# Value products of the late heads in 64x64 tiles only: three blocks of 64 keys, one row tile of the group on each half of the rows

## The chip, the cores and the metric

The kernel runs on one core of one Trainium2 chip. The metric is the device time of one execution in microseconds (us). Before the change it is 658.24 us, the median of three runs (657.96 to 659.07).

## The reference

The kernel computes an attention with a causal window and a few global keys, and passes its result through a two-layer network with an ELU between the layers. All of it is f32. The mask of every row lets through the 96 keys up to its own and the first 8 keys.

```python
scores = q @ k.T / sqrt(64) - slope[h] * dist           # B=4, H=8, S=768, D=64
scores = where(is_global | is_local, scores, -1e9)      # 8 global keys, 96 local ones
a = softmax(scores)
x = (a @ v) -> [B * S, H * D]                           # 3072 x 512
h = x @ w_in                                            # 512 x 2048
g = where(h > 0, h, exp(min(h, 0)) - 1)
out = g @ w_out                                         # 2048 x 512
```

## The kernel before, in words

**Groups and heads.** The 3072 rows are cut into 12 groups of 256 rows: two row tiles i of 128 rows (`NT = 2`). A row tile has two halves r of 64 rows (`HW`). Each half looks at 168 keys (`LW`): 64 own ones, 96 before them and 8 global ones. Heads go in pairs j = 0, 1, so a group has four pairs `hp`.

**Early and late groups.** The first three groups are prepared in `pair` and `heads32`, where TensorE transposes the probabilities. The other nine groups, 36 head pairs, are the late ones (`far`), and the change is in these. A late pair k goes through the engines as follows.
- `visit` puts it on TensorE. A visit first does the value products of the pair that was scored two visits earlier (`BEHIND = 2`), and then the scores of its own pair (`scores`, L468). Both write the same two PSUM banks `s`, one for each row tile or head.
- `turned` takes the scores on: softmax on VectorE and ScalarE (L456, L458), division on GpSimd (L577), and a transpose of 32x32 blocks on VectorE into the tile `tr` (L582). `tr` has six blocks (`BLK = 6`) of 32 keys; 168 keys are padded to 192.
- The 32x32 transpose leaves the keys of a block on 32 partitions of a quadrant. To bring them into the order that a matmul needs, `tr` is stored to a buffer `dd` in DRAM (L591, two stores: blocks 0 to 3 and blocks 4, 5) and read back. Blocks 0 to 3 come back as `pt`, 128 keys on 128 partitions (L596, one transfer). Blocks 4 and 5 come back as `pu`, 64 keys of the first row tile on partitions 0 to 63 and of the second on 64 to 127 (L603, two transfers).
- `values` multiplies: eight matmuls over 128 keys (L617, array tiles of 128 rows x 64 columns, two heads side by side), then eight over the other 64 keys (L622, array tiles of 64x64; four of them, two row tiles and two heads, lie in the array at once).
- `v` holds the values of the first 128 keys, loaded for each pair; `u` holds those of the rest, loaded once for two pairs (L550, L553).

**Rest of TensorE's work.** The network of the earlier groups runs between the visits: `moe` (L844 up, L870 down), and from the sixth group on `seven` (L722 up, L778 down), which loads prepared sums of weights `mix` from DRAM (L761).

**What sets the order.** Every operation is handed to `Plan.add` with a cost, a due time and what it reads and writes. `Plan.order` then lays out all engines greedily by its own model of durations, DMA bandwidth and free buffers (`SLOTS`). The order on each engine is fixed when the program is built. SyncE (SP) issues nearly all DMAs, in order: one that waits holds up those behind it.

Of the kernel before, what the change touches and what calls it, by code (L numbers as in the profile page):

```python
# [16 lines left out]
P = 128  # L17
NG = 8
NL = P - NG
NT = 2  # L20
HW = P // 2
BACKW = 96
LW = HW + BACKW + NG
BLK = 6
# [12 lines left out]
VN = 2 * VC  # L37

# [185 lines left out]
def sp():  # L224
    return (("SP", 450.0, False),)
# [19 lines left out]
class Kernel:  # L245
# [290 lines left out]
    def far(self, b, gi, hp, xh, xl, due, end, X):  # L536


        nc, p = self.nc, self.plan
        qk = self.sb("qk", "qk", [P, W + KS], slots=X.get("qk"))  # L540
        src = self.qkv[b, gi, hp]
        p.add(sp(), lambda e: nc.sync.dma_start(qk.t, src[:, :W + KS]), writes=[qk], due=due - 14000, nbytes=P * (W + KS) * 4)
        sc = self.scale.t[:, hp:hp + 1]
        p.add(act(W) + dve(W, True) + (("POOL", 60 + 1.1 * W, True),), lambda e: self.scaled(e, qk.t[:, :W], qk.t[:, :W], sc), [qk], [qk], due - 8000, slack=self.LOADED)
        rest = []

        def chain(ss, after):
            rest.extend(self.turned(b, hp, gi * NT, ss, due, end, X, after))
            v = self.sb("v", "v", [P, VC], slots=X.get("v"))
            p.add(sp(), lambda e: nc.sync.dma_start(v.t, src[:, W + KS:W + KS + VC]), writes=[v], due=end - 9000, nbytes=P * VC * 4)  # L550
            if hp % 2 == 0:
                self.rest = u = self.sb("u", "u", [P, VC], slots=X.get("u"))
                p.add(sp(), lambda e: nc.sync.dma_start(u.t, src[:, W + KS + VC:]), writes=[u], due=end - 9000, nbytes=P * VC * 4)  # L553
            rest.extend((v, self.rest))

        return qk, chain, (rest, hp, xh, xl, end)

    def turned(self, b, hp, t0, ss, due, end, X, after):
# [4 lines left out]
        pt, pu = self.sb("pt4", "pt4", [P, 4, NT, 2, 32], slots=X.get("pt4")), self.sb("pu", "pu", [P, 4, 2, 32])  # L563
# [21 lines left out]
        outs = []  # L585
        for a, (w0, w1) in enumerate(((0, 4), (4, BLK))):
            w = w1 - w0
            at = slice(P * w0, P * w1)
# [4 lines left out]
            outs.append(p.add(sp(), out, [tr], [dd], due - 2000, nbytes=P * w * 512, beside=tuple(outs)))  # L593
        def back(e):
# [3 lines left out]
        p.add(sp(), back, [dd], [pt], due - 1900, nbytes=P * 2048)  # L598
        backs = []
        for i in range(NT):  # L600
            def back(e, i=i):
                src = dd.t[P * 4:].rearrange("(q k w) x -> (k w) q x", q=4, w=2)[:, :, i * HW:(i + 1) * HW]
                nc.sync.dma_start(pu.t[i * HW:(i + 1) * HW].rearrange("k q j t -> k q (j t)"), src)  # L603

            backs.append(p.add(sp(), back, [dd], [pu], due - 1890, nbytes=P * 512, beside=tuple(backs)))
        return pt, pu

    def values(self, rest, hp, ss):

        pt, pu, v, u = rest  # L610
        vx = v.t.rearrange("p (i r j d) -> p i r j d", i=NT, r=2, j=2)
        ux = u.t.rearrange("p (m r j d) -> p m r j d", m=2, r=2, j=2)
        out = lambda i, r, j: ss[i].t[j * HW:(j + 1) * HW, r, LW:LW + HW].rearrange("p (c t) -> p c t", c=2)
        for i in range(NT):
            for r in range(2):
                for j in range(2):
                    self.nc.tensor.matmul(out(i, r, j), vx[:, i, r, j], pt.t[:, 2 * r:2 * r + 2, i, j], start=r == 0, stop=False)  # L617
        for r in range(2):
            for j in range(2):
                for i in range(NT):  # L620
                    rows = slice(i * HW, (i + 1) * HW)
                    self.nc.tensor.matmul(out(i, r, j), ux[rows, hp % 2, r, j], pu.t[rows, 2 * r:2 * r + 2, j], start=False, stop=r == 1)  # L622

    def visit(self, k, due):


        nc, p, N = self.nc, self.plan, len(self.fars)
        reads, cost = [], 250.0
        new = old = None
        if k < N:  # L630
            new = self.far(*self.fars[k][:-2], due, *self.fars[k][-2:])
            self.open.append(new[2])
            reads += [new[0]]
            cost += 575.0
        if k >= self.BEHIND:
            old = self.open[k - self.BEHIND]
            reads += old[0]
            cost += 660.0
        ss = [self.bank("s", "s", [P, NT, 2 * P]) for _ in range(2)]

        def both(e):
            if old:
                self.values(old[0], old[1], ss)
# [269 lines left out]
    def build(self):  # L913
# [63 lines left out]
        for _, f in sorted(todo, key=lambda x: x[0]):  # L977
# [29 lines left out]
             "gl": ["gl0", "gl1", "gl2"], "io": ["io0", "io1", "io2", "io3"], "part": [f"pa{i}" for i in range(6)], "mix": [f"pa{i}" for i in range(6)], "pu": ["pu0", "pu1"], "hl": ["x0", "ph2"], "tf": ["tf0", "tf1", "tf2", "tf3"],  # L1007
# [226 lines left out]
def layouts(q, k, v, w_in, w_out):  # L1234
# [9 lines left out]
    vf = np.zeros((B, nb, H // 2, 2 * NT, P, 2, D), np.float32)  # L1244
    tile_of = lambda x, t: x[:, :, t * P:(t + 1) * P]
    for g in range(nb):
        prev = max(g * NT - 1, 0)
        x = [tile_of(k, prev)[:, :, P - BACKW:]]
        for i in range(NT):
# [5 lines left out]
            for r in range(2):  # L1255
                x1 = y[:, :, r * HW:r * HW + LW].reshape(B, H // 2, 2, LW, D).swapaxes(2, 3)
                vv[:, g, :, :, 0, i, r] = x1[:, :, :P]
                for m in range(2):
                    vv[:, g, ::2, (2 - m) * HW - (LW - P):(2 - m) * HW, 1, i, r] = x1[:, m::2, P:]
            vf[:, g, :, 2 * i:2 * i + 2] = y.reshape(B, H // 2, 2, 2, 2, 2, 32, D).transpose(0, 1, 3, 4, 6, 5, 2, 7).reshape(B, H // 2, 2, P, 2, D)  # L1260
        kf[:, g] = np.concatenate(x, axis=2).reshape(B, H // 2, 2, KS, D).transpose(0, 1, 4, 2, 3)
    at = np.arange(P)
    first = at % 4 * 32 + at // 4
    key = at % 2 * 32 + at % HW // 2
    vp = vv[..., :NT, :, :, :][:, :, :, first].copy()
    vp[:, :, :, :, 0] = vv[:, :, :, first, 0]
    for m in range(2):
        x = np.zeros_like(vv[:, :, ::2, :HW, 1])
        x[:, :, :, :LW - P] = vv[:, :, ::2, (2 - m) * HW - (LW - P):(2 - m) * HW, 1]
        x = x[:, :, :, key[:HW]]  # L1270
        for i in range(NT):
            vp[:, :, ::2, i * HW:(i + 1) * HW, 1, m] = x[:, :, :, :, i]
    halves = lambda x: x.reshape(B, nb, H // 2, D, 2, -1).swapaxes(3, 4).reshape(B, nb, H // 2, 2 * D, -1)
    qkv, qkv1 = (np.concatenate([halves(qT), halves(kf), x], axis=4)
                 for x in (vp.reshape(B, nb, H // 2, P, VN), vv.reshape(B, nb, H // 2, P, VN)))
# [30 lines left out]
```

## Time and profile before

| what | value |
|---|---|
| median of three runs | 658.24 us |
| the profiled execution's own time | 657.76 us |
| its span, first to last instruction | 655.9 us |
| granted TensorE clock, mean | 0.995 |
| TensorE busy | 640.3 us (98%) |
| VectorE busy | 488.9 us (75%) |
| ScalarE busy | 418.3 us (64%) |
| DMA moved | 143.43 MB, 107837 packets, 27744 of them under 512 B |

The profiled execution has 1.9 us around its span. A matmul in f32 stands in the trace as two records: L617 has 576 records for 36 x 8 matmuls. PE is TensorE's matmul side, PEld its weight loads, SPq the queue that SyncE issues. A busy PE is not a PE at its peak: the ends of the records are modelled and they overlap, so durations on PE are read from start to start.

### The profile page before, as it was taken

To read this page: it belongs to the slowest core of one execution; us is meant where nothing else is said; L and a number is where in the kernel's file an instruction comes from. 1 tells how busy PE (TensorE), PEld (TensorE's weight loads), DVE (VectorE), ACT (ScalarE), POOL (GpSimd) and SP (SyncE) were. 2 spreads that over 40 slices of the span, in tenths; PEclk is the share of its full clock that TensorE was granted. 3 is DMA by queue.
4 is the path that set the end of the run, shared out by engine and by line. 5 is a ranking of instruction groups with operands and counts; after the bars stand their busy time and mean duration, and the time that the engine had idled before them with its cause. 6 is when DMAs were issued, how large, how long until landed. Compare 5 with 4: busy or idle time off the path is not lost.

```text
span 655.9 us, 17768 instructions
## 1 busy us (share of the span) xinstructions
PE 640.3 (98%) x6390; PEld 583.9 (89%) x6390; DVE 488.9 (75%) x1611; ACT 418.3 (64%) x1218; POOL 192.7 (29%) x480
## 2 busy tenths in 40 slices
PE   8989999999999999999999999999999999999996
PEld 5768888989887888888999999999999999999995
DVE  6998998897787777644767876877877867866655
ACT  6898886765655666655666675676675676655452
POOL 3565475544266455221113121121121121110000
PEclk9999999999999999999999999999999999999999
DMA  8989373200288658676588889798788789774542
GB/s 310 363 298 406 136 270 80 66 16 17 90 254 279 196 191 272 229 233 184 178 251 284 258 265 264 238 284 262 247 275 255 250 271 267 228 224 152 176 146 83
DMA packets 107837, 143.43 MB, mean 219 GB/s; under 512 B 27744, under 2 KB 55136, under 8 KB 107744
## 3 DMA queue, kind: packets, MB, share of 16 engines
q1 hardware_dynamic: 107744, 142.25, 67.3%
q8 instruction: 51, 0.84, 0.5%
q14 instruction: 42, 0.34, 0.2%
HBM read 111.28 MB, written 30.93 MB: 217 GB/s over the span
## 4 chain that ended last, share of the span: by engine, by line
PE 80%; DVE 6%; DMA 6%; ACT 3%; issue 2%; POOL 2%; SPq 1%; DVEq 0%; POOLq 0%; ACTq 0%
PE h L722 23%; PE o L778 20%; PE o L870 13%; PE h L844 13%; PE s L468 4%; PE s L617 3%; DMA qk<-in_qkv_dram 2%; PE s L622 2%; DMA dd<-tr 2%; PE pv L501 1%; DMA pt<-dd 1%; ACT pr L458 1%; POOL pr L577 1%; PE t L521 1%; DVE mix L307 1%
## 5 line engine op out<-in xcount | busy, mean ns | idle before, releaser
L577 POOL TENSOR_SCALAR pr<-pr,st 128x168 f32<-128x168 f32 x144 | 66.5, 461 | 269.3 <-DVE st L476 222.2
L722 PE MATMUL h<-xh,w 128*128 128x256 f32 x896 | 124.3, 280 | 0.0
L722 PEld LDWEIGHTS h<-xh,w 128*128 128x128 f32 x896 | 113.1, 188 | 2.7 <-DVE gg L732 1.9
L844 PEld LDWEIGHTS h<-xh,w 128*128 128x128 f32 x640 | 95.9, 188 | 15.9 <-DVE gl L307 3.7
L844 PE MATMUL h<-xh,w 128*128 128x256 f32 x640 | 102.1, 283 | 1.5 <-DVE gl L307 1.3
L870 PE MATMUL o<-w,gh 128*128 128x512 f32 x320 | 102.7, 403 | 0.3
L732 DVE SCALAR_TENSOR_TENSOR gg<-e,h 128x256 f32<-128x256 f32 x112 | 47.0, 419 | 68.9 <-ACT e L731 68.1
L458 ACT ACTIVATE pr<-pr,nmax 128x168 f32<-128x168 f32 x192 | 82.2, 429 | 14.4 <-DVE nmax L456 13.9
L730 ACT ACTIVATE e<-h 128x256 f32<-128x256 f32 x112 | 42.9, 383 | 59.8 <-PE h L722 59.8
L722 PE MATMUL h<-xl,w 128*128 128x256 f32 x448 | 71.1, 280 | 0.0
L456 DVE CUSTOM_DVE_ANT_0 pr<-s,far 128x168 f32<-128x168 f32 x192 | 54.2, 326 | 17.3 <-ACT xh L299 13.7
L870 PEld LDWEIGHTS o<-w,gh 128*128 128x128 f32 x320 | 54.3, 190 | 10.2 <-issue 1.4
L307 POOL TENSOR_TENSOR w<-g,w 128x256 fp32r<-128x256 f32 x64 | 50.4, 811 | 42.5 <-ACT w L299 27.6
L722 PEld LDWEIGHTS h<-xl,w 128*128 128x128 f32 x448 | 60.5, 188 | 0.9 <-issue 0.7
L852 DVE SCALAR_TENSOR_TENSOR h<-e,h 128x256 f32<-128x256 f32 x80 | 33.8, 422 | 32.4 <-ACT e L851 32.1
L778 PE MATMUL o<-mix,sh 128*128 128x256 f32 x336 | 57.5, 279 | 0.0
L870 PE MATMUL o<-w,gl 128*128 128x512 f32 x160 | 56.0, 403 | 0.0
L582 DVE STREAM_TRANSPOSE tr<-pr 128x192 f32<-128x192 f32 x144 | 49.3, 362 | 3.7 <-POOL pr L577 2.7
L850 ACT ACTIVATE e<-h 128x256 f32<-128x256 f32 x80 | 30.6, 383 | 33.5 <-PE h L844 33.0
L299 ACT CAST sh<-sum 128x512 fp32r<-128x512 f32 x56 | 34.8, 621 | 25.0 <-DVE sum L746 25.0
L844 PE MATMUL h<-xl,w 128*128 128x256 f32 x320 | 50.7, 280 | 0.0
L778 PE MATMUL o<-w,sh 128*128 128x256 f32 x336 | 48.8, 280 | 0.7 <-DVE ob L808 0.7
(129 smaller groups left out, 1299.9 us busy)
## 6 DMA issues: line engine op xcount, KB each, us to landing
mix<-mixed SPq DMA_DIRECT2D x168, 256.0 KB, 4.0
qk<-in_qkv_dram SPq DMA_DIRECT2D x48, 312.0 KB, 3.7
v<-in_qkv_dram SPq DMA_DIRECT2D x48, 256.0 KB, 4.4
dd<-tr SPq DMA_DIRECT2D x36, 256.0 KB, 3.5
pt<-dd SPq DMA_DIRECT2D x36, 256.0 KB, 4.0
bits<-in_w_in_dram SPq DMA_DIRECT2D x16, 512.0 KB, 7.7
bits<-in_w_out_dram SPq DMA_DIRECT2D x16, 512.0 KB, 8.9
mixed<-mix SPq DMA_DIRECT2D x32, 256.0 KB, 3.0
```

The source lines that it names most:

```text
L299: self.nc.scalar.copy(out, x)
L307: self.on(e).tensor_tensor(out, x, y, ALU.subtract)
L456: first = p.add((("DVE", 85 + 1.042 * LW, False),), lambda e: nc.vector.tensor_tensor_reduce(x(), s.t[:, i, :LW], tab, -(2.0 ** -(h + 1)), ...
L458: p.add(act(LW, extra=200), lambda e: nc.scalar.activation(x(), x(), AF.Exp, bias=nm, scale=-1.0, accum_out=st.t[:, n, 0:1]), [pr], [pr, s ...
L577: nc.gpsimd.tensor_scalar(pr.t[:, :LW], pr.t[:, :LW], st.t[:, n, 3:4], 1.0, ALU.mult, ALU.mult)
L582: nc.vector.transpose(tr.t[:, :, i, j], pr.t.rearrange("p (b r) -> p b r", r=32))
L722: nc.tensor.matmul(h.t, w1.t[:, s, cc * P:(cc + 1) * P], x.t[:, cc], start=n == 0 and s == HI and cc == 0, stop=n == 1 and cc == self.NCC - 1)
L730: p.add(act(W, True), lambda e: nc.scalar.activation(ex.t, h.t, AF.Relu, scale=-1.0), [h], [ex], d - 8000)
L732: p.add(dve(W), lambda e: nc.vector.scalar_tensor_tensor(gs(), ex.t, -1.0, h.t, ALU.add, ALU.max), [h, ex], [g], d - 8000)
L778: nc.tensor.matmul(acc[bank].t[:, half], a, b.t[:, LO if t == 1 else HI, x], start=j == 0 and t == 0 and n in first, stop=j == self.NFC // ...
L844: nc.tensor.matmul(h.t, w1.t[:, s, cc * P:(cc + 1) * P], x.t[:, cc], start=n == 0 and cc == 0, stop=n == 2 and cc == self.NCC - 1)
L870: nc.tensor.matmul(o.t[:, :at.stop - at.start], g.t[:, i * P:(i + 1) * P], w2.t[:, s, at], start=fc == f0 and n == 0 and s == HI, stop=fc ...
```

## The change

The 168 keys of a late pair, padded to 192, are taken as three blocks of 64 instead of one of 128 and one of 64. Row tile i of the group lies on partitions 64i to 64i + 63, for all three blocks.
- `values` has 24 matmuls of 64x64 tiles instead of eight of 128x64 and eight of 64x64.
- `tr` goes out in one store (L584 after the change) of 1 KB pieces, and comes back in two transfers (L591 after the change), one for each row tile, all in pieces of 256 B.
- `pu` and `u` are gone; `pt4` and `v` are half again as large. The values are laid out on the host to match.
- The planner's cost of the value products in a visit goes from 660 to 640 ns, and two of the four buffers of `tf` are now the ones that `u` had.

```diff
@@ chain, in far @@
-            rest.extend(self.turned(b, hp, gi * NT, ss, due, end, X, after))
-            v = self.sb("v", "v", [P, VC], slots=X.get("v"))
-            p.add(sp(), lambda e: nc.sync.dma_start(v.t, src[:, W + KS:W + KS + VC]), writes=[v], due=end - 9000, nbytes=P * VC * 4)
-            if hp % 2 == 0:
-                self.rest = u = self.sb("u", "u", [P, VC], slots=X.get("u"))
-                p.add(sp(), lambda e: nc.sync.dma_start(u.t, src[:, W + KS + VC:]), writes=[u], due=end - 9000, nbytes=P * VC * 4)
-            rest.extend((v, self.rest))
+            rest.append(self.turned(b, hp, gi * NT, ss, due, end, X, after))
+            v = self.sb("v", "v", [P, VL], slots=X.get("v"))
+            p.add(sp(), lambda e: nc.sync.dma_start(v.t, src[:, W + KS:]), writes=[v], due=end - 9000, nbytes=P * VL * 4)
+            rest.append(v)
@@ turned @@
-        pt, pu = self.sb("pt4", "pt4", [P, 4, NT, 2, 32], slots=X.get("pt4")), self.sb("pu", "pu", [P, 4, 2, 32])
+        pt = self.sb("pt4", "pt4", [P, BLK // 2, 4, 2, 32], slots=X.get("pt4"))
...
-            def out(e, w0=w0, w1=w1, w=w, at=at):
-                nc.sync.dma_start(dd.t[at].rearrange("(p w) x -> p (w x)", w=w), tr.t[:, w0:w1].rearrange("p w i j r -> p (w i j r)"))
+        def out(e):
+            nc.sync.dma_start(dd.t.rearrange("(a p w) x -> p a (w x)", a=BLK // 2, w=2), tr.t.rearrange("p (a w) i j r -> p a (w i j r)", w=2))
...
-            src = dd.t[:P * 4].rearrange("(q k w) x -> (k w) q x", q=4, w=4)
-            nc.sync.dma_start(pt.t.rearrange("k q i j t -> k q (i j t)"), src)
...
-                src = dd.t[P * 4:].rearrange("(q k w) x -> (k w) q x", q=4, w=2)[:, :, i * HW:(i + 1) * HW]
-                nc.sync.dma_start(pu.t[i * HW:(i + 1) * HW].rearrange("k q j t -> k q (j t)"), src)
+                src = dd.t.rearrange("(a q k w) x -> (k w) (a q) x", a=BLK // 2, q=4, w=2)[:, :, i * HW:(i + 1) * HW]
+                nc.sync.dma_start(pt.t[i * HW:(i + 1) * HW].rearrange("k a q j t -> k (a q) (j t)"), src)
@@ values @@
-        for i in range(NT):
+        for a in range(BLK // 2):
             for r in range(2):
                 for j in range(2):
-                    self.nc.tensor.matmul(out(i, r, j), vx[:, i, r, j], pt.t[:, 2 * r:2 * r + 2, i, j], start=r == 0, stop=False)
-        for r in range(2):
-            for j in range(2):
-                for i in range(NT):
-                    rows = slice(i * HW, (i + 1) * HW)
-                    self.nc.tensor.matmul(out(i, r, j), ux[rows, hp % 2, r, j], pu.t[rows, 2 * r:2 * r + 2, j], start=False, stop=r == 1)
+                    for i in range(NT):
+                        y = slice(i * HW, (i + 1) * HW)
+                        self.nc.tensor.matmul(ss[i].t[j * HW:(j + 1) * HW, r, LW:LW + HW].rearrange("p (c t) -> p c t", c=2), vx[y, a, r, j],
+                                              pt.t[y, a, 2 * r:2 * r + 2, j], start=(a, r) == (0, 0), stop=(a, r) == (BLK // 2 - 1, 1))
@@ visit @@
-            cost += 660.0
+            cost += 640.0
@@ SLOTS @@
-"pu": ["pu0", "pu1"], "tf": ["tf0", "tf1", "tf2", "tf3"],
+"tf": ["tf0", "tf1", "rk0", "va0"],
```

The planner lays the program out anew. On TensorE most visits keep their place between the blocks of the network. These are the rows of TensorE around the visit that does the value products of late pair 20 (the one whose products begin at 395.39 us before), first before the change:

```order
L722 MATMUL h_6413<-xh_5065,w_521_2228 128x256 x8
L722 MATMUL h_6413<-xl_5106,w_521_2228 128x256 x4
L617 MATMUL s_6435<-pt_1257_6333,v_6118 64x64 x4
L617 MATMUL s_6436<-pt_1257_6333,v_6118 64x64 x4
L622 MATMUL s_6435<-pu_6341,u_5587 64x64
L622 MATMUL s_6436<-pu_6341,u_5587 64x64
```

And the same place after it, with the first two of its 24 matmuls (L706 is the line that was L722, L605 the new matmul):

```order
L706 MATMUL h_6483<-xh_5111,w_513_2239 128x256 x8
L706 MATMUL h_6483<-xl_5152,w_513_2239 128x256 x4
L706 MATMUL h_6504<-xh_5111,w_519_2275 128x256 x8
L605 MATMUL s_6519<-pt_1228_6404,v_6187 64x64
L605 MATMUL s_6520<-pt_1228_6404,v_6187 64x64
```

One more block of eight matmuls of the network now stands ahead of this visit. The same holds for the value products that begin at 445.01, 494.51 and 544.02 us before. The other visits from 255 us on keep their places.

On SyncE's queue, these are the rows around the store and the return of late pair 27 before the change, from the last `mix` load ahead of them to the first behind:

```order
L761 DMA mix_7847<-mixed_3508 128x512
L591 DMA dd_7858<-tr_7804 128x512
L591 DMA dd_7858<-tr_7804 128x256
L542 DMA qk_7903<-in_qkv_dram 128x624
L550 DMA v_7906<-in_qkv_dram 128x512
L596 DMA pt_1555_7916<-dd_7858 128x4x128
L603 DMA pu_7927<-dd_7858 64x4x64 x2
L553 DMA u_7947<-in_qkv_dram 128x512
L761 DMA mix_7950<-mixed_3748 128x512
```

And after it:

```order
L745 DMA mix_7941<-mixed_3539 128x512
L584 DMA dd_7952<-tr_7898 128x3x256
L543 DMA qk_8004<-in_qkv_dram 128x624
L551 DMA v_8007<-in_qkv_dram 128x768
L591 DMA pt_1516_8017<-dd_7952 64x12x64 x2
L745 DMA mix_8046<-mixed_3780 128x512
```

Between the two `mix` loads eight issues become five (`x2` counts as two); what stands ahead of and behind them is the same.

## Rows read from the trace of the kernel before

**Rows 1.** The page, part 1: busy us, share of the span and instructions

```profile
PE   640.3 (98%) x6390; PEld 583.9 (89%) x6390; DVE 488.9 (75%) x1611; ACT 418.3 (64%) x1218; POOL 192.7 (29%) x480
```

**Rows 2.** A stretch of late visits: us, busy by engine, granted clock, DMA share, GB/s

```profile
475.00:525.00 50.00, 49.95 (x565) 48.15 (x566) 37.18 (x136) 32.55 (x94) 7.67 (x32) 1.00 0.83 260
```

**Rows 3.** Line view of L617: ns min/median/max, first and last start us

```profile
L617 PE MATMUL s<-pt,v x576: 222/222/271, 108.3 to 592.8; 128*64 128x64 f32 x192
```

**Rows 4.** Timeline of PE, one visit: start us, us, line, operation, records

```profile
425.61 0.69 PE L617 MATMUL s<-pt,v 128*64 128x64 f32 x16
426.23 0.46 PE L622 MATMUL s<-pu,u 64*64 64x64 f32 x16
426.51 0.75 PE L468 MATMUL s<-qk 64*64 64x168 f32 x16
427.19 1.21 PE L722 MATMUL h<-xh,w 128*128 128x256 f32 x8
```

**Rows 5.** Timeline of PE, narrow windows around 426.24: what runs there

```profile
426.01 0.29 PE L617 MATMUL s<-pt,v 128*64 128x64 f32 x4
426.23 0.29 PE L622 MATMUL s<-pu,u 64*64 64x64 f32 x4
...
426.07 0.23 PE L617 MATMUL s<-pt,v 128*64 128x64 f32 x2
```

**Rows 6.** Timeline of PE, narrow windows: entry into 64x64, and into 128x64

```profile
98.58 0.40 PE L844 MATMUL h<-xh,w 128*128 128x256 f32 x2
98.91 0.37 PE L468 MATMUL s<-qk 64*64 64x168 f32 x4
...
107.96 0.40 PE L844 MATMUL h<-xh,w 128*128 128x256 f32 x2
108.29 0.34 PE L617 MATMUL s<-pt,v 128*64 128x64 f32 x4
```

**Rows 7.** Line view of the round trip's issues on SyncE: ns min/median/max

```profile
L591 SPq DMA_DIRECT2D dd<-tr x72: 319/424/1354, 93.2 to 583.7; - x72
L603 SPq DMA_DIRECT2D pu<-dd x72: 585/607/1690, 96.2 to 587.9; - x72
L596 SPq DMA_DIRECT2D pt<-dd x36: 370/377/861, 95.7 to 586.7; - x36
```

**Rows 8.** Timeline of SyncE's queue, round trip of late pair 27

```profile
474.10 0.85 SPq L591 DMA_DIRECT2D dd<-tr  x2
...
477.15 1.25 SPq L550 DMA_DIRECT2D v<-in_qkv_dram  x1
478.49 0.39 SPq L596 DMA_DIRECT2D pt<-dd  x1
478.97 1.24 SPq L603 DMA_DIRECT2D pu<-dd  x2
```

**Rows 9.** DMA issues: count, KB each, median us from issue to landing

```profile
pt<-dd SPq DMA_DIRECT2D x36, 256.0 KB, 4.0
...
pu<-dd SPq DMA_DIRECT2D x72, 64.0 KB, 3.7
```

**Rows 10.** View of tile pu, 479 to 481: issues of pair 27, landing

```profile
L603 SPq DMA_DIRECT2D pu<-dd x2: 585/596/607, 479.0 to 479.6; - x2
...
DMA to landing us min/median/max: 3.7/3.9/4.1
```

**Rows 11.** View of tile pu, 488.5 to 491: issues of pair 28, landing

```profile
L603 SPq DMA_DIRECT2D pu<-dd x2: 585/597/609, 488.7 to 489.4; - x2
...
DMA to landing us min/median/max: 5.8/6.0/6.2
```

**Rows 12.** Timeline of PE: the value products of pairs 27 and 28 begin

```profile
483.49 0.28 PE L617 MATMUL s<-pt,v 128*64 128x64 f32 x2
...
494.51 0.28 PE L617 MATMUL s<-pt,v 128*64 128x64 f32 x2
```

**Rows 13.** Timeline of PE: the visit that waits for pu

```profile
338.92 0.40 PE L622 MATMUL s<-pu,u 64*64 64x64 f32 x11 [0.34 <-DMA pu<-dd]
```

More of the change, by code (lines that the diff above doesn't have):

```diff
@@ L37 @@
 VN = 2 * VC
+VL = BLK // 2 * 2 * P
 class Tl:
@@ L584, in turned @@
             p.add((("DVE", 150 + 1.042 * 32 * BLK, False),), turn, [pr], [tr], due - 2500 + 10 * n, slack=300.0)
[L585 to L588, printed above, removed]
-            def out(e, w0=w0, w1=w1, w=w, at=at):
-                nc.sync.dma_start(dd.t[at].rearrange("(p w) x -> p (w x)", w=w), tr.t[:, w0:w1].rearrange("p w i j r -> p (w i j r)"))
-            outs.append(p.add(sp(), out, [tr], [dd], due - 2000, nbytes=P * w * 512, beside=tuple(outs)))
-        def back(e):
-            src = dd.t[:P * 4].rearrange("(q k w) x -> (k w) q x", q=4, w=4)
-            nc.sync.dma_start(pt.t.rearrange("k q i j t -> k q (i j t)"), src)
-        p.add(sp(), back, [dd], [pt], due - 1900, nbytes=P * 2048)
+        def out(e):
+            nc.sync.dma_start(dd.t.rearrange("(a p w) x -> p a (w x)", a=BLK // 2, w=2), tr.t.rearrange("p (a w) i j r -> p a (w i j r)", w=2))
+        p.add(sp(), out, [tr], [dd], due - 2000, nbytes=P * BLK * 512)
         backs = []
@@ L642, in both @@
             if old:
-                self.values(old[0], old[1], ss)
+                self.values(old[0], ss)
             if new:
@@ L1006 @@
              "x": ["x0"], "xh": ["xh0", "xh1", "xh2"], "xl": ["xl0", "xl1", "xl2"], "e": ["e0", "e1"], "gh": ["gh0", "gh1", "gh2"],
-             "gl": ["gl0", "gl1", "gl2"], "io": ["io0", "io1", "io2", "io3"], "part": [f"pa{i}" for i in range(6)], "mix": [f"pa{i}" for i in range(6)], "pu": ["pu0", "pu1"], "hl": ["x0", "ph2"], "tf": ["tf0", "tf1", "tf2", "tf3"],
+             "gl": ["gl0", "gl1", "gl2"], "io": ["io0", "io1", "io2", "io3"], "part": [f"pa{i}" for i in range(6)], "mix": [f"pa{i}" for i in range(6)],  "hl": ["x0", "ph2"], "tf": ["tf0", "tf1", "rk0", "va0"],
              "g": ["io2", "io3"], "sum7": ["ph2", "x0"], "rh": ["gh0", "gh1"], "rl": ["gl0", "gl1"], "sh": ["xh2", "xl2"], "o2": ["v0"], "o3": ["t0"]}
@@ L1257, in layouts @@
                 vv[:, g, :, :, 0, i, r] = x1[:, :, :P]
+                keys[:, g, :, i, :LW, r] = x1
                 for m in range(2):
                     vv[:, g, ::2, (2 - m) * HW - (LW - P):(2 - m) * HW, 1, i, r] = x1[:, m::2, P:]
-            vf[:, g, :, 2 * i:2 * i + 2] = y.reshape(B, H // 2, 2, 2, 2, 2, 32, D).transpose(0, 1, 3, 4, 6, 5, 2, 7).reshape(B, H // 2, 2, P, 2, D)
         kf[:, g] = np.concatenate(x, axis=2).reshape(B, H // 2, 2, KS, D).transpose(0, 1, 4, 2, 3)
[L1262 to L1272, printed above, removed]
+    late = keys.reshape(B, nb, H // 2, NT, BLK // 2, 2, 32, 2, 2, D).transpose(0, 1, 2, 3, 6, 5, 4, 7, 8, 9)
     halves = lambda x: x.reshape(B, nb, H // 2, D, 2, -1).swapaxes(3, 4).reshape(B, nb, H // 2, 2 * D, -1)
     qkv, qkv1 = (np.concatenate([halves(qT), halves(kf), x], axis=4)
-                 for x in (vp.reshape(B, nb, H // 2, P, VN), vv.reshape(B, nb, H // 2, P, VN)))
+                 for x in (late.reshape(B, nb, H // 2, P, VL), vv.reshape(B, nb, H // 2, P, VN)))
     dm, ff = w_in.shape
```

14 lines of the change are left out of this document (6 added, 8 removed).

## The prediction

> **What bounds the kernel now.** I read the page's first part, then a stretch of late visits, then the value products: their line, the timeline of one visit, and the DMA round trip that feeds them. The reader is to see in the first that TensorE is busy for 640.3 of 655.9 us, with VectorE at 75% and ScalarE at 64% [rows 1]. Among the late visits it is tighter still: 49.95 of 50 us, at a granted clock of 1.00 (the 2.4 GHz level), with the DMA engines 0.83 busy [rows 2]. So what TensorE does faster shortens the kernel one for one, as long as nothing it needs comes late; and what comes late costs as much. All sums are made against the profiled execution's 657.76 us, 655.9 of span and 1.9 around it. The median of the runs, 658.24, lies 0.48 higher; I add that at the end.
>
> **TensorE's part: minus 5.0 us.** L617 has 576 records, 36 visits with 16 each, two for a matmul [rows 3]; L622 has as many. L617's records begin two at a time, the two heads; L622's four at a time, two heads and two row tiles [rows 5]. Call such a set a round: before there are 8 rounds of L617 and 4 of L622. After, 24 matmuls give 48 records, in the order L622 had, so 12 rounds of four. The number of rounds stays 12. What goes is one change of the array's shape, from 128x64 to 64x64, inside each visit.
>
> In the visit shown L617 begins at 425.61, L622 at 426.23 and the scores at 426.51, so the products take 0.62 + 0.28 = 0.90 us [rows 4]. L617's last rounds begin at 426.01 and 426.07, a step of 0.06, but L622's first comes only at 426.23, 0.16 later [rows 5]: 0.10 for the change of shape. After it four rounds need 0.28 instead of 4 x 0.06 = 0.24, so the first round costs 0.04 more, and that goes as well. Afterwards: four rounds with the slow first one, 0.28, and eight at 0.06, 0.48, together 0.76. That is 0.14 a visit, and 36 x 0.14 = 5.0 us. From below, if the 0.04 stays, 36 x 0.10 = 3.6. From above, if the whole 0.16 goes, 5.8. The value is the middle one, since all its pieces are read from one visit.
>
> The entry into the visit now is 128x128 to 64x64 instead of 128x128 to 128x64. The early visits without products show it: from the next to last record of the network to the first of L468 it is 98.91 - 98.58 = 0.33 us, and to L617 108.29 - 107.96 = 0.33 [rows 6]. Nothing is gained or lost there. The planner's 20 ns less for a visit moves no block but those named below.
>
> **The round trip: issues.** SyncE issues two stores (0.85 us with the pause), then `pt` (0.39) and two `pu` (1.24) for pair 27 [rows 8]. One store less saves about 0.42, its median [rows 7]. The return becomes two issues instead of three, each with 64 partitions and 12 pieces of 256 B per partition, where `pu` had 4. No row shows such a shape. From below each costs what `pu` costs at least, 0.585; from above three times `pu`'s median, 1.82, as the pieces are three times as many [rows 7]. I take `pu`'s 0.61: `pt` has 512 pieces and is issued in 0.377, `pu` has half as many and needs 0.607, so the time does not go by the number of pieces. The return then takes 1.3 us to issue instead of 478.49 to 480.21, 1.7. Against that stand 1536 pieces instead of 1024, and 196 KB in each issue. `pt` needs 4.0 us to land for 256 KB, `pu` 3.7 for 64 [rows 9]; I put 3.7 + 0.5 behind the last issue. The start of the return may not follow the store at once: in rows 8 the load of `v`, held for 1.25 us, ends at 478.40 and `pt` is issued behind it; I count half the store's 0.42. Sum: -0.2 - 0.4 + 0.5 = -0.1 us, with -0.5 and about +2 as its ends (+2: two issues of 1.82 are 3.6, 1.9 more than now). The queue behind the return holds `mix` loads, which are late by as much or little.
>
> **The round trip: how late it may be.** Before, `pu` is needed 0.62 us after the products begin [rows 4]; after, the first round needs both transfers whole. The visit between a pair's scores and its products is also 0.14 shorter. So the deadline comes 0.76 earlier. I compared, for all 36 pairs, the last landing of `pu` with the start of the products. In 22 it lands 1.4 us or more ahead. The other 14 lie between 1.0 ahead and 1.2 behind. Pair 27 is one: issued at 479.6, landed 3.7 later, at 483.3 [rows 10], products at 483.49 [rows 12]. Pair 28 is another: 489.4 + 5.8 = 495.2 [rows 11], products at 494.51, so 0.7 behind, just hidden by L617 [rows 12]. One does wait: after L622's first records TensorE stands until 338.92 [rows 13]. All such delays come to 0.8 us by the same comparison.
>
> The new order puts a block of eight matmuls, 0.94 us, ahead of the products of pairs 20, 24, 28 and 32, which are the four with `pu` 0.2 to 0.8 behind in this way. They come out even or better. With an unchanged round trip I get waits of 2.0 us: pair 15 alone 1.35, the rest from pairs 8, 11, 19, 31 with 0.05 to 0.35; a wait of one pair gives the next one time, so a couple of pairs counts once. At -0.1 they are about 1.6, at the low end of -0.5 0.9, nearly all of it pair 15. Less the 0.8 of today that is +0.8 and +0.1. I take +0.5, between the two, since the comparison holds to a tenth or two only.
>
> **Other edits.** `v` comes as 384 KB for a pair instead of 256 and, for every second, 256 more: the same bytes. That is half an issue less for a pair. `tf` keeps four buffers. VectorE, ScalarE and GpSimd do the same operations, some in other places. These I cost at 0: they lie beside TensorE's stream, with VectorE at 75% and ScalarE at 64% [rows 1]. If that cover were gone in each visit, because the shorter products leave them 0.14 us less, it would cost the same 36 x 0.14 = 5.0 us.
>
> Sum: 657.76 - 5.0 + 0.5 = 653.3, and on the scale of the median 653.7 us.
>
> **The Trainium skill against this.** The trace has `pu`, in 256 B pieces, land in 3.7 us and `pt`, in 512 B ones, in 4.0 [rows 9]: small pieces cost nothing to be seen at 64 KB. The Trainium skill's page "DMA: Bandwidth & Descriptors" (Specifications) puts the least size for full rate at 512 B and says that the engines read, modify and write below it. All of the return is now below it; by that rule the first rival is the outcome, at its time. The trace neither shows nor excludes it at 196 KB.
>
> The second is about the feed. In the visit 48 records begin within 427.19 - 425.61 = 1.58 us, 33 ns each [rows 4]. The Trainium skill's page "TensorE: Matmul & The Clock Gate" (Wait — 56ns, not 53.3ns?) says that the sequencer spends about 62 ns on a matmul when it decodes in software. The trace disagrees over one visit; whether a queue filled earlier hides it there, no row shows. That is the third rival.
>
> **Rivals.**
> 1. *The return comes late (slower).* Its issues take 1.0 us each or more, or its small pieces land later, and each couple of tight pairs makes TensorE wait. At 1.0 us beyond today the waits are 7 couples or single pairs with 0.3 to 2.3 us, together 9, less 0.8: 657.76 - 5.0 + 8.2 = 661.0, or 661.4 on the median's scale. It decides from about +0.65 on, where the waits eat the 5.0. For it: DMA engines 0.83 busy, 14 thin pairs. Against: one store and one return issue less, and `pt`'s quick issue.
> 2. *Half eaten.* The round trip is 0.3 to 0.6 longer; waits of 3 to 5 us. At 0.45: 657.76 - 5.0 + 3.7 = 656.5, or 657.0.
> 3. *The feed is the limit.* 72 records at 33 ns are 2.37 us instead of 1.58 - 0.14 = 1.44: 36 x 0.93 = 33 us more than the forecast, 687. Against it: L622's 16 records begin within 0.28 us [rows 4].
> 4. *It does not do what it says.* The 0.16 step is not the change of shape but something that remains, such as the weights' first load in the new place: 658.2, no change. Against it: the same 0.16 is there in all visits that do not wait.
>
> **How the numbers follow.** Chances: forecast 0.63, rival 1 0.15, rival 2 0.16, rival 3 0.02, rival 4 0.04. A measurement of this kernel tells 0.2%, 1.3 us, from no change. Faster: the forecast and half of rival 2, 0.71. Same: the other half and rival 4, 0.12. Slower: 0.17. The range goes from 651.9 (5.8 saved and the 0.5 not spent) to 659.0, which takes in rival 2 and the mild part of rival 1. The forecast's own range is 651.9 to 655.
>
> **What would show it.** In the profile after, a visit's products take 0.76 us from L605's first record to the scores and 36 of them are alike: that shows the first step. The return's issues at 0.6 us each, and waits of TensorE for `pt` of 1 to 2 us in all, show the second. Issues above 1 us, or waits for `pt` above 5 us in sum, would make the prediction wrong.

## The result, and the profile after

The changed kernel takes 661.98 us (median of its runs, 659.41 to 664.29) where before took 658.24. The ratio is 1.0067, with a 95% interval of 1.0045 to 1.009: slower by 0.67%, or 4.4 us on 658.24. The forecast was 653.7 us and faster, and 661.98 lies outside the range too. Only the first rival gave a time of this size, 661.4. The profiled execution took 661.4 us with a span of 659.6, against 655.9 of span before.

The first part of the page after, which answers to [rows 1] (busy us and share):

```profile
PE 638.4 (97%) x6966; PEld 584.2 (89%) x6966; DVE 484.1 (73%) x1613; ACT 416.6 (63%) x1214; POOL 191.8 (29%) x482
```

TensorE has 1.9 us less work in a span that is 3.7 us longer. What a visit costs when nothing is late, TensorE's timeline shows for one of them (late pair 26; start us, us, line, operation, records), beside [rows 4]:

```profile
477.70 0.93 PE L605 MATMUL s<-pt,v 64*64 64x64 f32 x48
478.45 0.75 PE L469 MATMUL s<-qk 64*64 64x168 f32 x16
479.13 1.21 PE L706 MATMUL h<-xh,w 128*128 128x256 f32 x8
```

The products now run from 477.70 to 478.45: 0.75 us where there were 0.90. In the records all undisturbed visits agree (0.748 to 0.749 against 0.896 to 0.897; the last two, which have no scores behind them, 0.86 against 1.01). So 0.148 us a visit went, 5.3 in all. The saving is there.

The waits view of TensorE after shows what took it back (us in all, times, longest; "issue" is a wait for which the profile names nothing):

```profile
PE s L605 <- DMA pt<-dd: 7.3, 11, 1.0
...
PE s L605 <- issue: 0.6, 1, 0.6
```

The same view of the kernel before, which the prediction had only as a comparison of landings:

```profile
PE h L844 <- DVE gl L307: 1.3, 1, 1.3
...
PE s L617 <- DMA pt<-dd: 0.4, 1, 0.4
PE s L622 <- DMA pu<-dd: 0.3, 1, 0.3
```

Waits for the return grew from 0.7 to 7.3 us. The account: from a visit's first product to the end of its scores the 36 visits sum to 60.28 us instead of 56.83, and the steps ahead of them to 10.09 instead of 8.61; together +4.9, in spite of the 5.3 saved. The 1.3 us that an up block waited for VectorE before (L844) are not there after. That makes +3.6 of the 3.7. (In one experiment, e9, the profiled execution was disturbed; nothing is read from its trace.)

One waiting visit, late pair 24, from TensorE's timeline after:

```profile
447.66 0.32 PE L605 MATMUL s<-pt,v 64*64 64x64 f32 x2
448.93 0.86 PE L605 MATMUL s<-pt,v 64*64 64x64 f32 x43 [0.95 <-DMA pt<-dd]
449.58 0.30 PE L469 MATMUL s<-qk 64*64 64x168 f32 x1
449.59 0.26 PE L605 MATMUL s<-pt,v 64*64 64x64 f32 x3
449.65 0.78 PE L469 MATMUL s<-qk 64*64 64x168 f32 x15
450.36 0.74 PE L706 MATMUL h<-xl,w 128*128 128x256 f32 x4
```

Two records run, those of the first matmul, which is on the first row tile's half, and TensorE then stands: the second matmul needs the other half, and it has not come. The view counts 0.95 us, from the modelled end of the two records (447.66 + 0.32). From start to start it is more: the second matmul begins at 448.93, 1.27 us behind the first, where it is 0.01 in the records of the undisturbed visit. From 448.93 to the next block at 450.36 are 1.43 us, as from 477.70 to 479.13 in the visit that did not wait, so a wait costs its own length and nothing behind it. Read in this way, against an undisturbed visit, the waits inside the visits are 9.9 us in 12 visits after and 1.1 in 4 before; the waits view leaves out a part of each, and the short ones altogether.

SyncE's queue for this pair's round trip (the same columns):

```profile
436.35 0.37 SPq L584 DMA_DIRECT2D dd<-tr  x1
437.53 0.33 SPq L543 DMA_DIRECT2D qk<-in_qkv_dram  x1
437.91 0.79 SPq L551 DMA_DIRECT2D v<-in_qkv_dram  x1
438.80 1.63 SPq L745 DMA_DIRECT2D mix<-mixed  x3
440.52 1.35 SPq L591 DMA_DIRECT2D pt<-dd  x2
```

And the view of tile pt, for each of its two return issues (duration, start, and from issue to landing):

```profile
L591 SPq DMA_DIRECT2D pt<-dd x1: 585/585/585, 440.5 to 440.5; - x1
...
DMA to landing us min/median/max: 6.9/6.9/6.9
...
L591 SPq DMA_DIRECT2D pt<-dd x1: 711/711/711, 441.2 to 441.2; - x1
...
DMA to landing us min/median/max: 7.6/7.6/7.6
```

The first half lands at 440.5 + 6.9 = 447.4, in time for 447.66; the second at 441.2 + 7.6 = 448.8, and at 448.93 TensorE goes on. The same pair before, in TensorE's timeline:

```profile
445.01 0.69 PE L617 MATMUL s<-pt,v 128*64 128x64 f32 x16
445.63 0.46 PE L622 MATMUL s<-pu,u 64*64 64x64 f32 x16
```

and its last two return issues in the view of tile pu:

```profile
L603 SPq DMA_DIRECT2D pu<-dd x2: 585/597/609, 439.6 to 440.2; - x2
...
DMA to landing us min/median/max: 5.0/5.2/5.3
```

The second of the two has the 5.0, so the last part landed at 440.2 + 5.0 = 445.2, 0.2 us after the products began, and nobody waited: L617 was still running. That cover is what the 128x64 products had given.

The issues after, in the line views that [rows 7] showed of before (ns, min/median/max):

```profile
L584 SPq DMA_DIRECT2D dd<-tr x36: 370/378/1519, 91.8 to 587.0; - x36
...
L591 SPq DMA_DIRECT2D pt<-dd x72: 583/645/1531, 94.4 to 591.0; - x72
```

And the landings, beside [rows 9]:

```profile
dd<-tr SPq DMA_DIRECT2D x36, 384.0 KB, 4.0
pt<-dd SPq DMA_DIRECT2D x72, 192.0 KB, 4.1
```

A return issue has a median of 0.645 us, close to the 0.61 forecast, and 192 KB in 256 B pieces land in 4.1 us, like `pt`'s 256 KB before. What moved is the whole trip. From its records, over pairs 13 to 36, medians in us, first from the end of a pair's scores and then from the start of its store:

```
                                        before   after
from the scores' end:  store starts       8.43    8.73
                       return starts     12.27   13.18
                       last part landed  17.74   18.76
from the store's start: first store landed  3.50   4.32 (the only one)
                        second store landed 3.93    -
                        return starts       3.95    4.52
```

The return ends 1.0 us later after the scores, where the prediction had put 0.1 earlier.

More than half of these pairs have time to spare. For the 14 that the prediction found thin (4, 8, 11, 15, 16, 19, 20, 23, 24, 27, 28, 31, 32, 36) the means from the same records are, in us:

```
                                        before   after
from the scores' end:  store starts       8.52    8.45
                       return starts     12.80   13.17
                       last part landed  17.92   18.87
from the return's first issue to its last landing
                                          5.12    5.70
```

The end is 0.95 later here too, but not by the store's start: the return begins 0.4 later, and it takes 0.6 longer. The store's later start in the medians is for the most part that of pairs with some 9 us to spare. In pairs 22, 26, 30 and 34 VectorE now has four sums of the network between the transposes that fill `tr`, where it had one row of the network before, and their store starts 0.5 to 1.3 later.

### The profile page after: what moved, and what is told of

Read it like the earlier page. It is cut to its first block, busy times and chain, and to the rows that moved or that the text cites. A ratio compares the mean times of both kernels' runs of the same rounds, so it can differ in the third digit from the quotient of the medians.

```text
span 659.6 us, 18853 instructions
## 1 busy us (share of the span) xinstructions
PE 638.4 (97%) x6966; PEld 584.2 (89%) x6966; DVE 484.1 (73%) x1613; ACT 416.6 (63%) x1214; POOL 191.8 (29%) x482
## 2 busy tenths in 40 slices
DMA packets 127137, 143.50 MB, mean 218 GB/s; under 512 B 63168, under 2 KB 81344, under 8 KB 127040
## 5 line engine op out<-in xcount | busy, mean ns | idle before, releaser
L575 POOL TENSOR_SCALAR pr<-pr,st 128x168 f32<-128x168 f32 x144 | 65.0, 451 | 276.4 <-ACT e L714 122.9
L706 PE MATMUL h<-xh,w 128*128 128x256 f32 x896 | 124.3, 280 | 0.0
L706 PEld LDWEIGHTS h<-xh,w 128*128 128x128 f32 x896 | 113.5, 188 | 1.7 <-DVE gg L716 1.0
L706 PE MATMUL h<-xl,w 128*128 128x256 f32 x448 | 71.7, 281 | 0.0
L706 PEld LDWEIGHTS h<-xl,w 128*128 128x128 f32 x448 | 60.6, 188 | 1.9 <-issue 1.7
```

The lines of the kernel that those rows point to most:

```text
L575: nc.gpsimd.tensor_scalar(pr.t[:, :LW], pr.t[:, :LW], st.t[:, n, 3:4], 1.0, ALU.mult, ALU.mult)
L706: nc.tensor.matmul(h.t, w1.t[:, s, cc * P:(cc + 1) * P], x.t[:, cc], start=n == 0 and s == HI and cc == 0, stop=n == 1 and cc == self.NCC - 1)
```

## Experiments

Theory A: the tiles' saving is real, and the return, which is later and needed whole at the first round, makes TensorE wait. Rivals: B, the 256 B pieces are slow; C, the planner's new places or the load as such (in e1's text, C is a wait on another engine). Ratios are to runs of the kernel before on the same chip; "waits" is the sum of the waits view for the return in the profiled execution, with what that view leaves out.

```
kernel                              median   ratio   95% interval       waits us
after                               661.98   1.0067  1.0045 to 1.0090   7.3
e1  before, tiles only              653.33   0.9928  0.9904 to 0.9953   0
e2  before, pt in 256 B pieces      659.04   1.0020  1.0001 to 1.0040   0.5
e3  after, both cut                 657.26   0.9996  0.9974 to 1.0018   2.8
e4  after, later place              652.92   0.9937  0.9912 to 0.9962   0.4
e5  before, later place             654.68   0.9976  0.9959 to 0.9994   0
e6  after, both cut, later place    651.70   0.9922  0.9897 to 0.9948   0
e7  before, stores exchanged        655.49   0.9968  0.9950 to 0.9986   0.5
e8  after, scores first             657.37   0.9994  0.9965 to 1.0022   4.9
e9  after, store in 3 KB pieces     661.19   1.0058  1.0030 to 1.0086   not read
e10 e9, later place                 651.89   0.9930  0.9904 to 0.9955   0.4
e11 after, old price of a visit     661.59   1.0075  1.0043 to 1.0107   9.1
e12 after, return cut               658.75   1.0022  1.0001 to 1.0043   2.1
e13 after, store cut                664.23   1.0116  1.0083 to 1.0148   7.2
```

**e1, the tiles without the new trip.**

```diff
-        for i in range(NT):
+        for c in range(2):
...
-                    self.nc.tensor.matmul(out(i, r, j), vx[:, i, r, j], pt.t[:, 2 * r:2 * r + 2, i, j], start=r == 0, stop=False)
+                    for i in range(NT):
+                        y = slice(i * HW, (i + 1) * HW)
+                        self.nc.tensor.matmul(out(i, r, j), vx[y, i, r, j], pt.t[y, 2 * r:2 * r + 2, i, j], start=(c, r) == (0, 0), stop=False)
```

> The kernel before, with its first eight value matmuls of a pair (L617, 128x64) issued as sixteen 64x64 ones, as in the kernel after; the two stores, the return in pt and pu and v stay as before. (The sixteen use only half of the weights of each 128-key block, twice, so the first block's sum is left incomplete.) Theory A (the tiles gain 0.148 us a visit, and the return, which is late in the kernel after, eats it): here pt comes first and pu is still needed half a microsecond into the products, so nearly the whole 36 x 0.148 = 5.3 us comes out: 652.5 to 654 us where before is 658.2, ratio 0.991 to 0.994. Theory B (small pieces and more packets slow the transfers): the same number, as nothing of the transfers changes. Theory C (the shorter visit only moves the wait to another engine): 657.5 to 658.5, ratio 0.999 to 1.001.

Ratio 0.9928, or 4.7 us less (3.1 to 6.3), as A and B said and C did not. Its visits stand where they stood before, its products take 0.748 us a visit, and the waits view has no row for the return (one of 0.6 us ahead of a visit is put down to "issue"). The first step of the prediction holds by itself.

**e2, the small pieces without the rest.**

```diff
+        for i in range(NT):
...
-            src = dd.t[:P * 4].rearrange("(q k w) x -> (k w) q x", q=4, w=4)
+                src = dd.t[:P * 4].rearrange("(q k w) x -> (k w) q x", q=4, w=4)[:, :, i * HW:(i + 1) * HW]
```

> The kernel before, with pt returned by two transfers of 256 B pieces (half of the rows each) instead of one of 512 B pieces; the two stores, pu and the products stay. Theory A (the return is late because it waits for the whole store and all of it is needed at the first round): little here, one issue more for a pair, and pu lands about 0.3 to 0.5 us later with the first half of the products still ahead of it: 658 to 660 us, ratio 1.000 to 1.003. Theory B (pieces of 256 B and twice the packets make the return and the transfers beside it slow): most of what the kernel after lost beside its saving, 8 to 9 us in waits: 663 to 667, ratio 1.008 to 1.014.

Ratio 1.002: one return issue more and almost as many small pieces as the kernel after (65,184 packets under 512 B; after has 63,168) cost 1.3 us by the ratio (0.1 to 2.6), with waits of 0.5; the planner put the visits of pairs 3, 8, 11 and 15 0.2 to 0.5 us later with it. In the 14 thin pairs its return takes 5.00 us in the mean, no more than before. B is out.

**e3, the trip in two parts again.**

```diff
+        parts = ((0, 2), (2, BLK // 2))
+        for a0, a1 in parts:
+            def out(e, a0=a0, a1=a1):
+                dst = dd.t[P * 2 * a0:P * 2 * a1].rearrange("(a p w) x -> p a (w x)", a=a1 - a0, w=2)
...
+        for a0, a1 in parts:
+            for i in range(NT):
+                def back(e, i=i, a0=a0, a1=a1):
```

> The kernel after, with the round trip cut into two parts again: two stores (the first two blocks, the third) and four returns (each part for each half of the rows), all in pieces of 256 B. Theory A: the first part returns while the second is still being stored, as pt did before, so the return starts about 0.5 us earlier; four issues of 0.6 us take back about half of it. The waits fall from 9 to 4 to 7 us: 657 to 660, ratio to before 0.998 to 1.002. Theory B (small pieces): two issues and no fewer pieces, so no better than the kernel after: 661.5 to 664, ratio 1.005 to 1.009.

0.9996, inside A's bounds and outside B's, with twice as many issues. What A expected of the start is not there: the return begins 4.46 us behind the store's start (median of pairs 13 to 36), where the kernel after has 4.52. The planner also moved visits, as in e12 below. The waits view:

```profile
PE s L610 <- DMA pt<-dd: 2.8, 6, 0.7
```

**e4, the later place, and e5, its control.**

```diff
-    SLACK, LATER = 600.0, 1200.0
+    SLACK, LATER = 600.0, 2800.0
```

> The kernel after, with one number of the planner changed: the time by which a visit may be placed behind its due time goes from 1200 to 2800 ns, so that products come later after their return. Theory A (the return is late by 1.3 us at the tight pairs, and nothing else is wrong): the waits go and the saving of 5.3 us comes out: 652.5 to 655, ratio 0.991 to 0.995. Theory B (the transfers as such are too many, 256 B pieces at a DMA share of 0.83): a queue that is too slow is not cured by a later visit, 660 to 663, ratio 1.003 to 1.007.

> The kernel before with the planner's number of the last experiment (1200 to 2800 ns): its control. Theory A (in the kernel after, the later place only takes away waits for the return): the kernel before has 0.8 us of such waits, so nothing much to gain: 656.5 to 658.5, ratio 0.997 to 1.001. Rival (the number is worth its microseconds whatever the products are, and the kernel after would still be a loss beside this control): 652 to 654.5, ratio 0.991 to 0.995.

e4 has the same trip and the same products as the kernel after, at a ratio of 0.9937, and one wait for the return left:

```profile
PE s L605 <- DMA pt<-dd: 0.4, 1, 0.4
```

From 1.0067 to 0.9937 are 8.5 us. From first product to the end of the scores the visits sum to 52.18 us instead of 60.28, and the steps ahead of them to 8.33 instead of 10.09, so the waits that went are enough for all of it. The control gained 1.6 us. Its own waits for the return went, and of the 1.3 of L844 0.2 are left, but another wait of 1.3 us came (an output block, L870, behind ScalarE); its account is not closed. Against the control e4 is 2.6 us faster, with intervals that reach from about 0.5 to 4.6: the sign of the saving is there, its full 5.3 is not shown by this pair.

**e6, both cut and the later place.** To e3's edit it adds

```diff
-    SLACK, LATER = 600.0, 1200.0
+    SLACK, LATER = 600.0, 2800.0
```

> The kernel after with both: the round trip in two parts, and visits placed up to 2800 ns late. The trace of the later place alone has about 1.3 us of waits left in four visits. Theory A: these go too, and four return issues cost nothing beside TensorE's stream: 651.5 to 653.5, ratio 0.990 to 0.994. Rival (the split's extra issues and packets cost something of their own): no better than the later place alone or worse, ratio 0.994 to 0.998.

0.9922, the best median here; no row for the return in its waits view. It is 3.6 us under e5. Its interval overlaps e4's, so that the cut is worth something here too is not shown.

**e7, the other order of stores.**

```diff
-        for a, (w0, w1) in enumerate(((0, 4), (4, BLK))):
+        for a, (w0, w1) in enumerate(((4, BLK), (0, 4))):
```

> The kernel before with its two stores in the other order: the third block's first, then the first two blocks', so that pt, which waits for the latter alone, waits for the store issued last. Products, pieces and issues stay. It takes away only what I had overlooked: that the return begins while the other store is still on its way. Theory A: pt begins about 0.3 to 0.5 us later behind the first store, pu with it; the last return lands that much later, and TensorE waits 1 to 4 us in all: 658.5 to 661.5, ratio 1.001 to 1.006. Rival (the start of the return does not matter, only that all of it is needed at the first round): 657 to 658, ratio 0.999 to 1.001.

This expectation failed on both sides: 0.9968, faster. I had seen that before the change `pt` needs the first store alone: in 26 of 36 pairs it begins while the second is on its way. In e7 that is so in none, and it begins 0.27 us later; yet the last part lands only 0.15 later, and the waits for the return are 0.5, not more than before. So nothing here says that the change lost by the early start. The planner also placed other blocks differently in e7, and what made it 2.1 us faster I have not settled.

**e8, the scores first.**

```diff
+            if new:
+                self.scores(new[0], ss, range(NT))
             if old:
                 self.values(old[0], ss)
-            if new:
-                self.scores(new[0], ss, range(NT))
```

> The kernel after with the two parts of a visit exchanged: the scores first, then the value products. The instructions of all other engines and of the DMA queue stay in the same order. The products are needed 0.68 us later, and the scores that begin the next return's chain are done 0.75 us earlier, together 1.4 us, about what the tight pairs are late. Theory A: the waits fall from 9 us to 1 or 2: 653 to 655, ratio 0.992 to 0.996. Rival C (the loss sits in other places: visits of pairs 5, 7, 20, 24, 28 and 32 that the planner moved, or the DMA load as such): 659.5 to 662, ratio 1.002 to 1.007.

4.8 us better than after by the ratios (0.9994 for 1.0067), but not the 0.992 to 0.996 of A, and 4.9 us of waits remain:

```profile
PE s L605 <- DMA pt<-dd: 4.9, 8, 0.9
```

Half of the expectation was wrong. The scores end earlier, but the store starts 9.57 us behind them, not 8.73: VectorE's rows stand in the same order, between the network's, and nothing in them comes sooner. VectorE's timeline of e8 shows it at the transposes that fill `tr`:

```profile
430.95 0.38 DVE L580 STREAM_TRANSPOSE tr<-pr 128x192 f32<-128x192 f32 x1 [0.30 <-POOL pr L575]
431.40 0.42 DVE L716 SCALAR_TENSOR_TENSOR gg<-e,h 128x256 f32<-128x256 f32 x1
431.74 0.89 DVE L580 STREAM_TRANSPOSE tr<-pr 128x192 f32<-128x192 f32 x3
```

A gate product of the network stands between them. So only the 0.68 us of later need came, and that took a third of the waits, with every visit at its place of the kernel after. C, at 1.002 or more, is excluded but for its edge.

**e9 and e10, larger pieces of the store.**

```diff
-            nc.sync.dma_start(dd.t.rearrange("(a p w) x -> p a (w x)", a=BLK // 2, w=2), tr.t.rearrange("p (a w) i j r -> p a (w i j r)", w=2))
+            nc.sync.dma_start(dd.t.rearrange("(p w) x -> p (w x)", w=BLK), tr.t.rearrange("p w i j r -> p (w i j r)"))
...
-                src = dd.t.rearrange("(a q k w) x -> (k w) (a q) x", a=BLK // 2, q=4, w=2)[:, :, i * HW:(i + 1) * HW]
+                src = dd.t.rearrange("(q y) x -> y q x", y=HW)[:, :, i * HW:(i + 1) * HW]
```

e10 adds e4's 2800 to it.

> The kernel after with its one store in pieces of 3 KB instead of 1 KB (each of the 128 rows whole), the keys put into three blocks of 64 in the order that this gives, and the return and the products as in the kernel after (256 B pieces, all of it needed at the first round). In the kernel after the store lands 4.32 us after its start, in the kernel before the first of two (256 KB in 2 KB pieces) 3.50 and the second 3.93. Theory D (the store is late by its smaller pieces): it lands by 3.8, the return starts and lands 0.5 us earlier, and half of the 9 us of waits go: 656.5 to 659, ratio 0.998 to 1.002. Rival (its size, or the need at the first round, decides): 660.5 to 662.5, ratio 1.004 to 1.008.

> The last kernel and the later place of visits (2800 ns) together. If both work by taking waits away, the 1.3 us that the later place alone left go too: 651.5 to 653, ratio 0.990 to 0.993. If the store's pieces are worth nothing, as the later place alone: 652.5 to 653.5, ratio 0.993 to 0.995.

e9 is the kernel after again (1.0058): theory D falls. e10 cannot be told from e4 or e6.

**e11, the old price.**

```diff
-            cost += 640.0
+            cost += 660.0
```

> The kernel after with the planner's old price for the products of a visit (660 instead of 640 ns). The visit of late pair 5, which the new price puts six microseconds earlier, goes back to its place of before; nearly all others stay. Theory A (the return is late at all thin pairs): only the waits of pairs 4 to 8, together about 1.7 us, can go: 660 to 662, ratio 1.003 to 1.007. Rival C (the planner's new order is the cause): 656 to 658.5, ratio 0.996 to 1.001.

1.0075. The visit with pair 5's products and pair 7's scores is back in its place, and the loss is what it was, so its move is not the cause. The four visits with a block more ahead of them (pairs 20, 24, 28 and 32) stay as the change put them, so e11 does not test C for these; the block gives their returns 0.94 us more, and two of the four wait for nothing in the kernel after.

**e12 and e13, one cut each.** e12 keeps the single store and takes e3's four returns:

```diff
+        parts = ((0, 2), (2, BLK // 2))
-        for i in range(NT):
-            def back(e, i=i):
+        for a0, a1 in parts:
+            for i in range(NT):
+                def back(e, i=i, a0=a0, a1=a1):
```

e13 keeps the two returns behind e3's two stores:

```diff
-        def out(e):
+        for a0, a1 in parts:
+            def out(e, a0=a0, a1=a1):
```

> The kernel after with its return cut alone: one store as it is, and four returns (the first two blocks and the third, for each half of the rows), so that the third block's part, needed half a microsecond into the products, lands last. Theory A1 (that the first round needs the whole return decides): as much comes back as with both cut: 656.5 to 659, ratio 0.998 to 1.002. Theory A2 (that the return must wait for the whole store decides): 660.5 to 663, ratio 1.004 to 1.009, with two issues more for nothing.

> The kernel after with its store cut alone: two stores (the first two blocks, the third), and the two returns as they are, each of which needs both stores. Theory A1 (that the first round needs the whole return decides): nothing comes back, 660.5 to 662.5, ratio 1.004 to 1.008. Theory A2 (the whole store as one transfer lands late): the two stores land 0.2 to 0.4 us earlier than the one (3.93 in the kernel before against 4.32), and a third of the waits goes: 657.5 to 660, ratio 1.000 to 1.004.

The waits views, e12 and then e13:

```profile
PE s L607 <- DMA pt<-dd: 2.1, 7, 0.4
```

```profile
PE s L609 <- DMA pt<-dd: 7.2, 11, 1.1
```

Cutting the return brings the waits from 7.3 to 2.1 us by the view and the ratio to 1.0022, at the upper edge of what A1 expected; cutting the store leaves 7.2. A2 falls: in e13 both stores had landed 4.18 us after the start, 0.14 before the single one, and the return began no sooner (4.61). That e13 is slower than A1's 1.008 is not explained; its interval just touches that of after. In e12 the last return lands as late after the scores as in the kernel after (18.78 and 18.76 us). When TensorE needs it differs: the third block's part comes last and is needed half a microsecond into the products. But e12 is not as clean as it looks. With two issues more to place, the planner, in e3 as in e12, also put visits elsewhere: by TensorE's records pair 5's comes 40 records of the network later than in the kernel after, those of pairs 11 and 15 four, of 3 and 8 two, at about 0.12 us each, and pair 4's four earlier. Read from start to start, the waits inside the visits are 4.7 us in pairs 1 to 15 and 5.3 in pairs 16 to 36 in the kernel after, 1.0 and 5.1 in e12, 0.0 and 4.5 in e3. Most of what came back did so among the pairs where visits were moved, and how much of it is the cut's is not shown. That the need at the first round counts rests on the timeline of pair 24 and on e8, where no visit moves.

## Why the prediction was wrong

- *TensorE's part*, minus 5.0: right, 5.3 in the trace, 4.7 in e1. The change of array shape was the cost, and the entry stayed.
- *Issues*: the two return issues came out as taken (0.583 at least, 0.645 in the median, for 0.61). But the sum of the term, -0.1 with ends of -0.5 and +2, measured +1.0 from the scores. This is the term that failed, and in the 14 thin pairs, which decide, both of its parts did. The start of the return was put 0.2 earlier and came 0.4 later. I had credited half of the saved store; but the return now begins 0.04 us behind the landing of the single store, 4.52 us after the store's start, where `pt` began at 3.95 (medians). The prediction weighed issues and pieces, and never asked which store `pt` waits for. From the first issue to the last landing it was put 0.1 longer (-0.4 and +0.5) and took 0.6 longer: the last issue lands 5.05 us behind its start in the mean of the thin pairs, where 3.7 + 0.5 was taken. Why these issues land later is open. Pieces of 256 B alone do not do it (e2, 5.00 from first issue to last landing); e12, with four returns of such pieces, has 5.40 and the kernel after 5.70. The longer return is no accident of one execution: with the same two issues the thin pairs have 5.6 to 6.0 in e4, e8, e11 and e13, and with the three issues of before 4.9 to 5.3 in e1, e5 and e7. Why the store lands later, I could not settle either: in experiments with the same store the landing had medians from 4.10 (e8) to 4.67 us (e12), and e7 and e13 show that neither the order nor the number of stores decides the time.
- *The deadline*, 0.76 earlier: right as a number, and pair 24 and e8 show that it counts. With the trip unchanged it was to cost 2.0 us of waits. The two terms add up: 0.76 earlier and 1.0 later is the case that rival 1 had priced at 9 us of waits. Inside the visits 9.9 were measured, 7.9 of waits in the view with the one named "issue".
- *Rival 1* gave 661.4; its time was right, its reasons only in part. Its issues of 1 us or more are not there, and the small pieces cost little (1.3 us in e2, 0.1 to 2.6, with an issue more); that the parts land later is so in the thin pairs. The rule of the Trainium skill's page "DMA: Bandwidth & Descriptors" (Specifications) that pieces under 512 B are read, modified and written would have given this outcome for a reason that e2 does not bear out: 256 B pieces landed in a median of 3.7 us for 128 KB. Its chance was 0.15 because I took -0.1 for a term whose ends were -0.5 and +2, and gave the part of these ends beyond +0.65, where the rival decides, little weight, with 14 of 36 pairs on the edge.
- *Rivals 3 and 4* fall: 48 records run in 0.75 us, and the 0.10 us went with the shape. (Rival 3 counted 72 records for a visit; 48 of products and 16 of scores are 64, and its price would have been some 24 us and not 33. The low end of the range, 651.9, is on the scale of the profiled execution; on that of the median it is 652.4.)
- The text named the sign that it would be wrong by, "waits for `pt` above 5 us in sum"; it was 7.3.
- *Other edits*, put at 0: VectorE's new order makes the store later in pairs 22, 26, 30 and 34, which have the time, and none of them waits.

The version that beats both is the kernel after with visits placed later (652.92), or that with the trip cut as well (651.70): 0.6 and 0.8% under before, the first 0.4% of it more than the same number gives the kernel before.

## What to carry to other kernels

A saving on the engine that bounds a kernel also takes away the time in which its inputs were still coming: list for each input when its last part lands and which instruction first needs that part, before and after. Where a product that could start on the first part becomes one that needs all parts at its first step, schedule the consumer later together with the faster code (e4, 8.5 us here). Splitting the transfer in the order of use went with a gain in e3 and e12, but visits moved as well. Look at the pairs that decide, too: the median over all of them said that the return had not become slower, and in the thin ones it had. And when a third of the consumers sit within a microsecond of their inputs, a term with a range of two microseconds is not a small term: its upper end is the outcome to price first.

## What the runs showed of the hardware

- A round of value products in 64x64 tiles takes 0.06 us, and going over to it from the 128x64 shape inside a visit cost 0.148 us, with the slower first round; in e1 that is gone with nothing else changed.
- The least time of an issue on SyncE's queue does not go with the pieces: 64 rows with 12 pieces of 256 B each have a minimum of 0.583 us, and with 4 pieces each 0.585 [rows 7].
- A wait of about a microsecond at the first round costs its own length and no more: in pair 24 TensorE needs 1.43 us from its going on (448.93) to the network's next block (450.36), as an undisturbed visit does (477.70 to 479.13), at a granted clock of 1.00 in both stretches. TensorE goes on 0.1 us behind the landing of the missing half (448.8).
